# Half-row matmuls in the first feed-forward layer of a fused attention and feed-forward block

## The chip, the cores and the metric

The kernel runs on one core of a Trainium2 chip. The metric is the time of one execution on the device in microseconds (us), here the median of three runs.

## The reference

The input x has 2048 tokens (S) of 576 values (D). It is normalised per token, and the result goes to two branches that are added to x:

```python
x = A_x
xn = _layernorm(x, axis=-1)
return x + _A_ref(xn, A_wqkv, A_wo) + _B_ref(xn, B_w1, B_b1, B_w2)
```

Branch A is attention with 32 heads over 8 earlier positions at distances of 2. Branch B, in which the change lies, is a dense layer from 576 to 4608, Mish, and a dense layer back:

```python
h = jnp.einsum("bsd,df->bsf", x, w1) + b1
sp = jnp.log1p(jnp.exp(-jnp.abs(h))) + jnp.where(h > 0, h, jnp.zeros_like(h))
act = h * jnp.tanh(sp)
return jnp.einsum("bsf,fd->bsd", act, w2)
```

All inputs are float32.

## The kernel before, in words

**Precision.** A float32 operand is split into a high part, rounded to the format in which TensorE multiplies in one pass, and a low part, the difference. A product is three matmuls: high by high, low by high, high by low.

**The rest.** 576 is 4 x 128 + 64. The 64 left over are put on all 128 partitions: the host repeats the last 64 rows of the weights (`dup`, L1560), and `transpose_split` (L67) stores the transposed activations with their high part in partitions 0 to 63 and their low part in partitions 64 to 127 (L84 to L87). One matmul with the repeated high weights then gives high by high and low by high at once; a second one with the low weights gives high by low, and low by low beside it. These two matmuls are `rest` (L665 to L668).

**Halves, blocks, quads.** The tokens are done in two halves (hf) of 1024, each of two blocks (b) of 512, whose transposed activations are the tiles XTs[hf, b]: slots 0 to 3 high parts, 5 to 8 low parts, slot 4 the rest, and in block 1 also slot 9, the rest of block 0 less that of block 1. The hidden layer's 4608 columns are 36 groups of 128; a quad takes two groups and both blocks of a half, so there are 18 quads in a half and 36 in all. A quad makes its 2 x 2 blocks of h with Strassen and Winograd's seven products in place of eight: `m1_part` (L719) has six parts. Part 0 makes the first and second product, part 1 the third, parts 2 and 3 add to the first bank, part 4 finishes the third bank, part 5 the first. `prod` (L658) is one product over 256 inputs: six matmuls 512 wide. Each quad has four rests of two matmuls: in part 0 on bank 2, in part 3 on bank 1, in part 4 on bank 3, in part 5 on bank 1 (slot 9).

**Banks and evictions.** `bank` (L654) takes one of four PSUM buffers (tag h). `take` (L690) has ScalarE copy bank 1 as it then is into a tile (c11, c21 or c22; L695). `mish` (L697) puts its work off to the next item of the plan (`pend`, or `late` for the first quad): VectorE adds a bank to the copy (L706), ScalarE applies Mish (L707) and casts to the high part (L712), and GpSimd subtracts for the low part (L713). In part 3 of the kernel before, mish of block (1,1) reads bank 3, which part 4 goes on to write. In the first nine quads of the second half the results stay whole in `raw_act` slots, and a second Strassen form (`p_item`, L839) takes them up later.

**The order of work.** `plan` (L1139) is a list of items written out by hand: projections (`qkv_item`, `z_part`), first-layer parts, second-layer items (`m2_pair` L752, `p_item` L839, `m2_cols` L865) and output projections (`wo_part`). In the usual quad second-layer items of the quad before stand between parts 2, 3, 4 and 5. `quad` (L1227) has the orders; the first quad of each half takes its parts as 0, 2, 1, 3, 5, 4. Weight loads, splits and the attention's steps on the other engines are hung on items by `before` (L1148). On each engine the program order is the order of issue (L1544 to L1550).

Of the kernel before, what the change touches and what calls it, by code (L numbers as in the profile page):

```python
# [8 lines left out]
F32 = mybir.dt.float32  # L9
# [8 lines left out]
P = 128  # L18
# [21 lines left out]
def block_kernel(ctx: ExitStack, tc: tile.TileContext, x, wq, wo, w1, b1, w2, mask, out):  # L40
    nc = tc.nc
# [22 lines left out]
    for k in range(30):  # L64
        nc.tensor.transpose(warm[:, (k % 4) * P:(k % 4 + 1) * P], ident, ident)

    def transpose_split(src, dst, col, extra=None, pair=False):  # L67
        n = next(tpn)
        if pair:
            ta, tb = (ps.tile([P, 512], F32, tag="out", bufs=4, name=f"tt{k}_{n}") for k in range(2))  # L70
        else:
            ta = ps.tile([P, 512], F32, tag="h", bufs=4, name=f"ta_{n}")
            tb = ps.tile([P, 512], F32, tag="h", bufs=4, name=f"tb_{n}")
        for k in range(KT):
            nc.tensor.transpose(ta[:, k * P:(k + 1) * P], src[:, k * P:(k + 1) * P], ident)  # L75
        nc.tensor.transpose(tb[:, 0:P], src[:, KT * P:(KT + 1) * P], ident)
        if extra is not None:
            nc.tensor.transpose(tb[:, P:2 * P], extra, ident)
        tav = ta.rearrange("p (k t) -> p k t", k=KT)
        hi = dst[:, 0:KT, col:col + P]  # L80
        nc.scalar.copy(hi, tav)  # L81
        nc.vector.tensor_sub(dst[:, 5:5 + KT, col:col + P], tav, hi.bitcast(F32))
        e = 1 if extra is None else 2
        hr = dst[:, KT:KT + 5 * e - 4:5, col:col + P]  # L84
        tbv = tb.rearrange("p (k t) -> p k t", k=KT)[:, 0:e]
        nc.scalar.copy(hr, tbv)
        nc.vector.tensor_sub(hr[64:P], tbv[64:P], hr[64:P].bitcast(F32))  # L87

    XTs = {}
    rems = {}  # L90
# [93 lines left out]
    def ln_transpose(hf, b, jj):  # L184
        if jj == 0:
            XTs[hf, b] = sb.tile([P, 9 + b, TB], F32R, tag=f"xt{b}", bufs=1, name=f"xt_{hf}_{b}")
        xn = xns[hf, b * JB + jj]
        if (b, jj) == (0, 0):
            rems[hf] = sb.tile([P, JB, P], F32, tag="tt", bufs=2, name=f"rem_{hf}")
        rem = rems[hf][:, jj, :]  # L190
        if b == 0:
            nc.gpsimd.tensor_copy(rem, xn[:, KT * P:])
        else:
            nc.gpsimd.tensor_tensor(out=rem, in0=rem, in1=xn[:, KT * P:], op=ALU.subtract)
        transpose_split(xn, XTs[hf, b], jj * P, rem if b else None, (hf, b) == (1, 0) and jj < 3)

    def raw_load(src, width, name):
        raw = sb.tile([P, 5 * P], F32, tag="raw", bufs=4, name=f"r{name}")
# [452 lines left out]
    cur = {}  # L651
    late = []

    def bank(hf, q, n):  # L654
        cur[n] = ps.tile([P, TB], F32, tag="h", bufs=4, name=f"h{n}_{hf}_{q}")
        return cur[n]

    def prod(ph, wt, off, X, hi, lo, first, last):  # L658
        seq = [(off + k, wl, xs + k) for k in range(2) for wl, xs in ((0, hi), (0, lo), (1, hi))]
        for i, (wk, wl, xs) in enumerate(seq):  # L660
            nc.tensor.matmul(ph, wt[:, wl, wk * P:(wk + 1) * P], X[:, xs, :],  # L661
                             start=first and i == 0, stop=last and i == len(seq) - 1,
                             skip_group_check=True)

    def rest(ph, wt, off, X, xs):  # L665
        for wl in range(2):
            nc.tensor.matmul(ph, wt[:, wl, off * P:(off + 1) * P], X[:, xs, :], start=False, stop=wl == 1,  # L667
                             skip_group_check=True)  # L668

    seven = lambda hf, q: hf == 1 and q <= 2 * OC  # L670
# [2 lines left out]
    def raw_act(q, b, j):  # L673
        if not rslot:
            for n in range(4):
                rslot["raw", n] = sb.tile([P, 5 * P], F32, tag="raw", bufs=4, name=f"ra{n}")
            for n in range(5):
                rslot["mn", n] = sb.tile([P, D], F32, tag="mn", bufs=5, name=f"rm{n}")
            for n in range(2):
                rslot["tt", n] = sb.tile([P, 4 * P], F32, tag="tt", bufs=2, name=f"rt{n}")  # L680
        tag, n = {(0, 0): (("raw", 0), ("raw", 1), ("raw", 2)), (1, 0): (("mn", 2), ("mn", 3), ("mn", 0), ("r3", 0)),
                  (0, 1): (("raw", 3), ("mn", 4), ("mn", 1)), (1, 1): (("tt", 0), ("tt", 1))}[b, j][q % {(1, 0): 4, (1, 1): 2}.get((b, j), 3)]
        if (tag, n) not in rslot:
            rslot[tag, n] = sb.tile([P, 2 * 432], F32, tag="r3", bufs=1, name="ra_r")
        rawact[q, b, j] = rslot[tag, n][:, 0:TB]
        owner[tag, n] = q, b, j
        where[q, b, j] = tag, n
        return rawact[q, b, j]

    def take(hf, q, name):  # L690
        if seven(hf, q):
            t = cur[name] = raw_act(q, *dict(c11=(0, 0), c21=(1, 0), c22=(1, 1))[name])
        else:
            t = cur[name] = sb.tile([P, TB], F32, tag="mn", bufs=5, name=f"{name}_{hf}_{q}")
        nc.scalar.copy(t, cur[1])  # L695

    def mish(hf, q, b, j, ph, t=None):  # L697
        f = 2 * (Q1[q] if hf else q) + j
        n = f"{hf}_{b}_{f}"
        fresh = t is None  # L700
        if fresh:
            t = raw_act(q, b, j) if seven(hf, q) else sb.tile([P, TB], F32, tag="mn", bufs=5, name=f"mn_{n}")

        def run():
            if not fresh:
                nc.vector.tensor_tensor(out=t, in0=ph, in1=t, op=ALU.add)  # L706
            nc.scalar.activation(t, ph if fresh else t, AF.Mish, bias=b1c[:, f:f + 1])  # L707
            if seven(hf, q):
                held_[q, f"A{b + 1}{j + 1}"] = f"A{b + 1}{j + 1}"
                return  # L710
            a = acts[hf, q, b, j] = sb.tile([P, 2, TB], F32R, tag=f"a{b}", bufs=(3, 2)[b], name=f"act_{n}")
            nc.scalar.copy(a[:, 0, :], t)  # L712
            nc.gpsimd.tensor_tensor(out=a[:, 1, :], in0=t, in1=a[:, 0, :].bitcast(F32), op=ALU.subtract)  # L713
        if q or b != j:
            pend.append(run)
        else:
            late.append(run)

    def m1_part(hf, q, part):  # L719
        X0, X1 = XTs[hf, 0], XTs[hf, 1]  # L720
        if part == 5 and late:
            for fn in late[::-1]:
                fn()
            late.clear()
        wa, wc, t0, t1 = (done.get((k, hf, q)) for k in ("wa", "wc", "t0", "t1"))
        if part == 0:
            prod(bank(hf, q, 1), wa, 0, X0, 0, 5, True, True)
            take(hf, q, "c11")
            prod(bank(hf, q, 2), wa, 2, X0, 2, 7, True, False)
            rest(cur[2], wa, 4, X0, 4)  # L730
            mish(hf, q, 0, 0, cur[2], cur["c11"])
        elif part == 1:
            prod(bank(hf, q, 3), t1, 0, X1, 0, 5, True, True)
        elif part == 2:
            prod(cur[1], t0, 2, Ss[hf, 1], 0, 2, False, True)
            take(hf, q, "c21")
        elif part == 3:
            prod(cur[1], t0, 0, Ss[hf, 0], 0, 2, False, False)
            rest(cur[1], wc, 2, X1, 4)
            take(hf, q, "c22")  # L740
        elif part == 4:
            prod(cur[3], t1, 2, X1, 2, 7, False, False)
            rest(cur[3], wa, 4, X1, 4)
            mish(hf, q, 1, 0, cur[3], cur["c21"])
        else:
            prod(cur[1], wc, 0, Ss[hf, 2], 0, 2, False, False)
            rest(cur[1], wc, 2, X1, 9)
            mish(hf, q, 0, 1, cur[1])
        if part == 3:
            mish(hf, q, 1, 1, cur[3], cur["c22"])  # L750

    def m2_pair(hf, q, b, p):  # L752
        for jj in (2 * p, 2 * p + 1):
# [403 lines left out]
    def mi(hf, q, part, alias=None):  # L1157
        add(("m", hf, q, part), lambda: m1_part(hf, q, part), alias=alias)
# [21 lines left out]
    def prologue():  # L1180
        for ns in ((0,), (1,), (2,), (3,), (4, 5), (6, 7)):
            ln_group(ns)
        hold(ln_stats(0))
        ln_root(0)
        first_cast(0, nc.gpsimd)()
        ln_newton(0)
        ln_stats(1)
        low1 = first_cast(1, nc.gpsimd)
        ln_norm(0)
        low1()  # L1190
        first_cast(2, nc.gpsimd)()
        ln_root(1)
        ln_newton(1)
        ln_transpose(0, 0, 0)
        first_cast(3, nc.gpsimd)()
        ln_norm(1)
        first_cast(4, nc.gpsimd)()
        ln_stats(2)
# [23 lines left out]
    def tr(b, jj):  # L1222
        add(("t", 1, b, jj), lambda: ln_transpose(1, b, jj))
# [273 lines left out]
    for n in range(2 * steps):  # L1497
# [4 lines left out]
        hf = n // steps  # L1502
# [86 lines left out]
```

## Time and profile before

| What | Value |
|---|---|
| Median of 3 runs | 1120.08 us (1119.49 to 1120.12) |
| Span of the profiled execution, first to last instruction | 1118.2 us |
| Outside that span, against the median | 1.9 us |
| Granted TensorE clock | 1.000 of full speed |
| Instructions | 18402 |
| DMA, all queues | 271.08 MB, mean 242 GB/s |

The profiled execution is known by its span alone. In the page's rows PE is TensorE's matmuls, PEld its weight loads, DVE VectorE, ACT ScalarE, POOL GpSimd, SP the engine that issues the DMAs. A group of instructions is shown as line, engine, operation, output<-input, shape and count, then busy time and mean duration, then the idle time ahead of them and what ended it. A timeline row has the start, the length of the whole merged stretch, the engine, the line, the operation and the count; what stands in brackets is the idle time ahead of it and what ended that. A row of one line's instructions has the shortest, median and longest duration in ns, and the first and last start in us. Matmuls are pipelined: the next one starts before the last has ended, so the lengths of neighbouring rows overlap.

### The profile page before, as it was taken

What the parts mean: (1) busy time and instruction counts of PE and PEld (TensorE: products, weight loads), DVE (VectorE), ACT (ScalarE), POOL (GpSimd) and SP (SyncE); (2) the same over time, 40 slices, a digit from 0 to 9 for tenths busy, and PEclk for the clock granted to TensorE, in tenths of its full rate; (3) what the DMA queues carried; (4) which work ended last, traced back from release to release, by engine and by line L of the source; (5) the groups of instructions that cost most, each with busy time, mean ns of one, the idle gap of its engine ahead of it and who ended that gap; (6) DMA issues with size and microseconds to landing.
All of it is one profiled execution on the core that took longest, in us unless ns stands there. A gap on an engine that the chain in (4) does not pass through costs nothing.

```text
span 1118.2 us, 18402 instructions
## 1 busy us (share of the span) xinstructions
PE 1109.2 (99%) x6630; PEld 1023.9 (92%) x6630; DVE 835.2 (75%) x1355; ACT 491.7 (44%) x892; POOL 777.4 (70%) x631
## 2 busy tenths in 40 slices
PE   8999999999999999999999999999999999999998
PEld 8999899999999999999999888989999999999998
DVE  6369788888888888887656566687866677776876
ACT  5544645544554545555233354343433343443332
POOL 2479777767689687685787346666789878668632
PEclk9999999999999999999999999999999999999999
DMA  6899695868767849666696797665655477576463
GB/s 200 284 311 313 227 357 205 294 227 282 260 241 265 273 169 342 226 240 215 208 332 234 240 378 254 225 200 188 220 192 190 173 266 270 207 258 243 160 217 108
DMA packets 147487, 271.08 MB, mean 242 GB/s; under 512 B 30114, under 2 KB 86724, under 8 KB 147396
## 3 DMA queue, kind: packets, MB, share of 16 engines
q1 hardware_dynamic: 147396, 269.91, 69.8%
q8 instruction: 52, 0.85, 0.3%
q14 instruction: 39, 0.32, 0.1%
HBM read 160.39 MB, written 109.48 MB: 241 GB/s over the span
## 4 chain that ended last, share of the span: by engine, by line
PE 94%; DVE 3%; POOL 1%; ACT 1%; issue 1%; DMA 0%; SPq 0%; DVEq 0%; POOLq 0%; ACTq 0%
PE h L661 30%; PE po L759 20%; PE pq L348 11%; PE po L872 10%; PE po L851 7%; PE h L667 6%; PE o L1060 4%; PE z L446 4%; POOL accP L860 1%; DVE accP L875 0%; POOL act L713 0%; DMA acc<-in_x 0%; PE ta L75 0%; DVE og L582 0%; POOL act L814 0%
## 5 line engine op out<-in xcount | busy, mean ns | idle before, releaser
L759 PEld LDWEIGHTS po<-w,act 128*128 128x128 f32 x1728 | 236.4, 188 | 6.0 <-POOL act L713 0.4
L759 PE MATMUL po<-w,act 128*128 128x288 f32 x1728 | 240.7, 295 | 0.1
L576 POOL TENSOR_TENSOR pv<-L,kv 128x576 f32<-128x576 f32 x128 | 176.3, 1477 | 38.5 <-DVE L L569 28.9
L713 POOL TENSOR_TENSOR act<-c,act 128x512 fp32r<-128x512 f32 x81 | 107.6, 1329 | 126.1 <-ACT act L712 124.4
L538 POOL TENSOR_TENSOR pr<-q,kv 128x576 f32<-128x576 f32 x120 | 184.2, 1564 | 7.7 <-DMA q<-q_d 6.0
L763 DVE TENSOR_TENSOR acc<-po,acc 128x288 f32<-128x288 f32 x288 | 120.0, 449 | 31.8 <-PE po L759 30.5
L348 PE MATMUL pq<-wq,xt 128*128 128x432 f32 x672 | 136.4, 361 | 1.2 <-ACT xt L81 1.2
L872 PEld LDWEIGHTS po<-w,act 128*128 128x128 f32 x960 | 131.1, 188 | 3.7 <-DVE accP L875 0.4
L872 PE MATMUL po<-w,act 128*128 128x288 f32 x960 | 133.8, 295 | 0.2
L348 PEld LDWEIGHTS pq<-wq,xt 128*128 128x128 f32 x672 | 125.0, 188 | 8.2 <-ACT xt L81 2.1
L707 ACT ACTIVATE c<-c,b1c 128x512 f32<-128x512 f32 x81 | 58.7, 725 | 130.6 <-DVE c L706 130.2
L661 PE MATMUL h<-S,t 128*128 128x512 f32 x432 | 110.4, 391 | 0.0
L661 PE MATMUL h<-xt,t 128*128 128x512 f32 x432 | 110.4, 391 | 0.0
L695 ACT COPY c<-h 128x512 f32<-128x512 f32 x81 | 47.5, 586 | 133.2 <-PE h L667 75.2
L582 DVE TENSOR_REDUCE og<-pv 128x144 f32<-128x1152 f32 x64 | 85.9, 1343 | 26.8 <-POOL pv L576 26.7
L661 PE MATMUL h<-xt,wa 128*128 128x512 f32 x432 | 104.1, 390 | 0.0
L543 DVE TENSOR_REDUCE L<-pr 128x64 f32<-128x1152 f32 x64 | 85.8, 1342 | 17.6 <-POOL pr L538 17.4
L875 DVE TENSOR_TENSOR accP<-po,accP 128x288 f32<-128x288 f32 x160 | 69.7, 454 | 38.9 <-PE po L872 37.4
L661 PEld LDWEIGHTS h<-xt,wa 128*128 128x128 f32 x432 | 80.9, 188 | 17.0
L851 PEld LDWEIGHTS po<-pw,u 128*128 128x128 f32 x672 | 92.2, 188 | 2.9 <-DVE u L805 0.7
L851 PE MATMUL po<-pw,u 128*128 128x288 f32 x672 | 93.7, 295 | 0.4 <-DVE u L805 0.4
L661 PEld LDWEIGHTS h<-xt,t 128*128 128x128 f32 x432 | 79.1, 188 | 14.7 <-DVE rt L706 0.2
(232 smaller groups left out, 1848.7 us busy)
## 6 DMA issues: line engine op xcount, KB each, us to landing
kv<-kv_d SPq DMA_DIRECT2D x64, 396.0 KB, 5.6
kept_t<-t SPq DMA_DIRECT2D x36, 512.0 KB, 5.2
t<-kept_t SPq DMA_DIRECT2D x36, 512.0 KB, 5.0
rw<-in_w SPq DMA_DIRECT2D x36, 320.0 KB, 4.5
kept_wa<-wa SPq DMA_DIRECT2D x18, 640.0 KB, 4.7
kept_w<-w SPq DMA_DIRECT2D x20, 576.0 KB, 4.1
wa<-kept_wa SPq DMA_DIRECT2D x18, 640.0 KB, 6.3
w<-kept_w SPq DMA_DIRECT2D x20, 576.0 KB, 4.7
```

Of the source, the lines that this page charges most:

```text
L348: nc.tensor.matmul(pq[:, 0:432], XT[:, xi, tok], wt[wi][:, hl, 0:432], start=i == 0, stop=i == len(seq) - 1)
L538: nc.gpsimd.tensor_tensor(out=pr[:, x:x + hh], in0=q[:, j0 + x:j0 + x + hh, None, :].to_broadcast([P, hh, W, CU]), in1=win(kt, 0, CU, j0 + ...
L543: nc.vector.tensor_reduce(L[:, k, j0:j0 + hj].rearrange("p j w h -> p (j w h)"), pr.rearrange("p j w (h d) -> p (j w h) d", h=2), axis=AX, ...
L576: nc.gpsimd.tensor_tensor(out=pr[:, x:x + hj].rearrange("p j d w -> p j w d"), in0=L[:, k, x:x + hj, :, h:h + 1].to_broadcast([P, hj, W, DH]),
L582: nc.vector.tensor_reduce(og[:, :, c0:c0 + DH], pr, axis=AX, op=ALU.add)
L661: nc.tensor.matmul(ph, wt[:, wl, wk * P:(wk + 1) * P], X[:, xs, :], start=first and i == 0, stop=last and i == len(seq) - 1, skip_group_ch ...
L713: nc.gpsimd.tensor_tensor(out=a[:, 1, :], in0=t, in1=a[:, 0, :].bitcast(F32), op=ALU.subtract)
L759: nc.tensor.matmul(po, acts[hf, q, b, j][:, al, tok], done["w2", hf, 2 * q + j][:, wl, c * HC:(c + 1) * HC], start=i == 0, stop=i == 5)
L763: nc.vector.tensor_tensor(out=t, in0=po, in1=t, op=ALU.add)
L851: nc.tensor.matmul(po, units[e, k, qq][:, al, tok], w[:, qq, wl, :], start=i == 0, stop=i == 5)
L872: nc.tensor.matmul(po, acts[hf, q, b, j][:, al, tok], done["w2", hf, 2 * q + j][:, wl, c * HC:(c + 1) * HC], start=i == 0, stop=i == 5)
L875: nc.vector.tensor_tensor(out=t, in0=po, in1=t, op=ALU.add)
```

## The change

The rest's low-weight matmul is taken out of `rest` and done on the 64 partitions that hold the high activations, with the 64 rows of low weights on the same partitions. Two of them stand next to each other, one on partitions 0 to 63 and one on 64 to 127, and write different banks. The term low by low drops out of the rest. For the lower half to be usable, slot 4 of block 1 is stored with its low part in partitions 0 to 63 and its high part in 64 to 127; slot 9 and block 0 stay as they were. The subtraction that stores the low parts, one instruction over both slots in block 1, becomes one for each slot.

The first pair, at the end of part 3, finishes the rests of bank 2 (from part 0) and bank 1 (part 3). The second, in part 4 or 5, whichever comes first, finishes those of bank 3 and of bank 1 with slot 9; the high-weight matmul of the latter moves there too. The Mish of block (0,0), which read bank 2 after part 0, moves to part 3, ahead of that of block (1,1).

```diff
+        for n in range(e):
+            lo = slice(0, 64) if low_first and n == 0 else slice(64, P)
+            nc.vector.tensor_sub(hr[lo, n], tbv[lo, n], hr[lo, n].bitcast(F32))
-        nc.vector.tensor_sub(hr[64:P], tbv[64:P], hr[64:P].bitcast(F32))
...
+    TOP, BOT = slice(0, 64), slice(64, P)
+
     def rest(ph, wt, off, X, xs):
-        for wl in range(2):
-            nc.tensor.matmul(ph, wt[:, wl, off * P:(off + 1) * P], X[:, xs, :], start=False, stop=wl == 1,
+        nc.tensor.matmul(ph, wt[:, 0, off * P:(off + 1) * P], X[:, xs, :], start=False, stop=False,
+                         skip_group_check=True)
+
+    def rest_low(*terms):
+        for rows, ph, wt, off, X, xs in terms:
+            nc.tensor.matmul(ph, wt[rows, 1, off * P:(off + 1) * P], X[rows, xs, :], start=False, stop=True,
                              skip_group_check=True)
...
             rest(cur[2], wa, 4, X0, 4)
-            mish(hf, q, 0, 0, cur[2], cur["c11"])
...
         elif part == 3:
             prod(cur[1], t0, 0, Ss[hf, 0], 0, 2, False, False)
             rest(cur[1], wc, 2, X1, 4)
+            rest_low((TOP, cur[2], wa, 4, X0, 4), (BOT, cur[1], wc, 2, X1, 4))
+            mish(hf, q, 0, 0, cur[2], cur["c11"])
             take(hf, q, "c22")
+            mish(hf, q, 1, 1, cur[3], cur["c22"])
+            cur["rests"] = True
         elif part == 4:
             prod(cur[3], t1, 2, X1, 2, 7, False, False)
+        else:
+            prod(cur[1], wc, 0, Ss[hf, 2], 0, 2, False, False)
+        if part > 3 and cur["rests"]:
+            cur["rests"] = False
             rest(cur[3], wa, 4, X1, 4)
+            rest(cur[1], wc, 2, X1, 9)
+            rest_low((BOT, cur[3], wa, 4, X1, 4), (TOP, cur[1], wc, 2, X1, 9))
+        if part == 4:
             mish(hf, q, 1, 0, cur[3], cur["c21"])
-        else:
-            prod(cur[1], wc, 0, Ss[hf, 2], 0, 2, False, False)
-            rest(cur[1], wc, 2, X1, 9)
+        if part == 5:
             mish(hf, q, 0, 1, cur[1])
-        if part == 3:
-            mish(hf, q, 1, 1, cur[3], cur["c22"])
```

More of the change, by code (lines that the diff above doesn't have):

```diff
@@ L65, in block_kernel, with transpose_split @@
         nc.tensor.transpose(warm[:, (k % 4) * P:(k % 4 + 1) * P], ident, ident)
-    def transpose_split(src, dst, col, extra=None, pair=False):
+    def transpose_split(src, dst, col, extra=None, pair=False, low_first=False):
         n = next(tpn)
@@ L194, in ln_transpose @@
             nc.gpsimd.tensor_tensor(out=rem, in0=rem, in1=xn[:, KT * P:], op=ALU.subtract)
-        transpose_split(xn, XTs[hf, b], jj * P, rem if b else None, (hf, b) == (1, 0) and jj < 3)
+        transpose_split(xn, XTs[hf, b], jj * P, rem if b else None, (hf, b) == (1, 0) and jj < 3, b == 1)
     def raw_load(src, width, name):
@@ L739, in m1_part @@
             rest(cur[1], wc, 2, X1, 4)
+            rest_low((TOP, cur[2], wa, 4, X0, 4), (BOT, cur[1], wc, 2, X1, 4))
+            mish(hf, q, 0, 0, cur[2], cur["c11"])
             take(hf, q, "c22")
+            mish(hf, q, 1, 1, cur[3], cur["c22"])
+            cur["rests"] = True
         elif part == 4:
             prod(cur[3], t1, 2, X1, 2, 7, False, False)
-            rest(cur[3], wa, 4, X1, 4)
-            mish(hf, q, 1, 0, cur[3], cur["c21"])
         else:
             prod(cur[1], wc, 0, Ss[hf, 2], 0, 2, False, False)
+        if part > 3 and cur["rests"]:
+            cur["rests"] = False
+            rest(cur[3], wa, 4, X1, 4)
             rest(cur[1], wc, 2, X1, 9)
+            rest_low((BOT, cur[3], wa, 4, X1, 4), (TOP, cur[1], wc, 2, X1, 9))
+        if part == 4:
+            mish(hf, q, 1, 0, cur[3], cur["c21"])
+        if part == 5:
             mish(hf, q, 0, 1, cur[1])
-        if part == 3:
-            mish(hf, q, 1, 1, cur[3], cur["c22"])
     def m2_pair(hf, q, b, p):
```

## Prediction

> **What bounds the kernel now.** I read the page's busy shares and slices first, then the list of waits, then the chain of work that ended last. They answer in that order whether an engine is full, whether it ever stands still, and which of its lines make up the time.
>
> ```profile
> span 1118.2 us, 18402 instructions
> PE 1109.2 (99%) x6630; PEld 1023.9 (92%) x6630; DVE 835.2 (75%) x1355; ACT 491.7 (44%) x892; POOL 777.4 (70%) x631
> PEclk9999999999999999999999999999999999999999
> PE warm L65 <- POOL ident masks.py:199: 1.3, 1, 1.3
> PE po L851 <- DVE u L805: 0.4, 1, 0.4
> PE 94%; DVE 3%; POOL 1%; ACT 1%; issue 1%; DMA 0%; SPq 0%; DVEq 0%; POOLq 0%; ACTq 0%
> PE h L661 30%; PE po L759 20%; PE pq L348 11%; PE po L872 10%; PE po L851 7%; PE h L667 6%; PE o L1060 4%; PE z L446 4%; POOL accP L860 1%; DVE accP L875 0%; POOL act L713 0%; DMA acc<-in_x 0%; PE ta L75 0%; DVE og L582 0%; POOL act L814 0%
> ```
>
> TensorE is busy 99% of the span at the full granted clock; its waits for others are single events of about a microsecond, and 94% of the chain is matmuls. So the time is the sum of the distances from one matmul's start to the next, and any matmul that goes, or runs beside another, shortens it. The line that the change touches, the 64-row rest (L667), holds 6% of the chain.
>
> What one such matmul takes must be read from starts, not from durations, because matmuls overlap. The timeline in the middle of the first half, around two rests of one quad, first TensorE's matmuls, then its weight loads, then ScalarE and VectorE:
>
> ```profile
> 296.34 1.53 PE L661 MATMUL h<-S,t 128*128 128x512 f32 x6
> 297.71 0.61 PE L667 MATMUL h<-xt,wc 128*128 128x512 f32 x2
> 298.16 3.34 PE L759 MATMUL po<-w,act 128*128 128x288 f32 x24
> 301.34 1.53 PE L661 MATMUL h<-xt,t 128*128 128x512 f32 x6
> 302.71 0.62 PE L667 MATMUL h<-xt,wa 128*128 128x512 f32 x2
> 303.16 0.42 PE L759 MATMUL po<-w,act 128*128 128x288 f32 x2
> ...
> 301.20 1.24 PEld L661 LDWEIGHTS h<-xt,t 128*128 128x128 f32 x6
> 302.48 0.41 PEld L667 LDWEIGHTS h<-xt,wa 128*128 128x128 f32 x2
> ...
> 298.36 0.59 ACT L695 COPY c<-h 128x512 f32<-128x512 f32 x1 [0.42 <-PE h L667]
> 299.71 0.72 ACT L707 ACTIVATE c<-c,b1c 128x512 f32<-128x512 f32 x1 [0.76 <-DVE c L706]
> ...
> 298.98 0.69 DVE L706 TENSOR_TENSOR c<-h,c 128x512 f32<-128x512 f32 x1
> ```
>
> Eight 512-wide matmuls start between 301.34 and 303.16: 1.82/8 = 0.227 us each. The 24 of 288 columns take (301.34-298.16)/24 = 0.132 us each. The rest's first weight load starts at 302.48, and the sixth matmul before it at 301.34 + 5 x 0.227 = 302.48 too: a load begins when the matmul ahead of its own begins, one ahead, and lies wholly under it. The second rest matmul of the earlier pair ends by its row at 297.71 + 0.61 = 298.32, and ScalarE, which had waited 0.42 us for it, starts at 298.36: a matmul's result really is there about 0.39 us after its start, though the next has long begun.
>
> **The change, part by part.** *Pairs.*
>
> ```profile
> L667 PE MATMUL h<-xt,wa x144: 388/389/397, 103.4 to 1029.0; 128*128 128x512 f32 x144
> L667 PE MATMUL h<-xt,wc x144: 388/390/405, 107.9 to 1034.0; 128*128 128x512 f32 x144
> ```
>
> These are 288 rest matmuls: four rests of two (high weights, low weights) in each of 36 quads. The 144 with low weights now use 64 rows each and stand in 72 pairs, one on the upper half of the rows and one on the lower, into different banks of PSUM. A pair costs 2 x 0.227 = 0.454 us now. No matmul of this trace uses 64 rows, so the pair's price is bounded. From above, as a plain sequence: 0.454, nothing won. From below, both at once: 0.227, which wins 72 x 0.227 = 16.3 us. Between lies what the rows suggest: two matmuls on different rows can stream together, but the lower one's weights are loaded one ahead, that is from the upper one's start. How soon a matmul can follow the start of its load is bounded by the densest streams of the trace: 0.132 us by the 288-wide matmuls above, and less by transposes:
>
> ```profile
> 1039.82 0.96 PE L872 MATMUL po<-w,act 128*128 128x288 f32 x6
> 1040.61 0.60 PE L906 MATMUL ot<-ident,o 128*128 128x128 f32 x4
> 1041.05 0.60 PE L922 MATMUL ot<-ident,o 128*128 128x128 f32 x4
> ```
>
> Four transposes take 1041.05 - 1040.61 = 0.44 us, 0.110 each. I take 0.132, the row with the same kind of operands. Then the lower half starts 0.132 after the upper, the next full matmul 0.227 behind that, the pair costs 0.359, and 72 x (0.454 - 0.359) = 6.8 us go. By the transposes it is 72 x (0.454 - 0.337) = 8.4 us.
>
> *Change of rows.* TensorE now goes from 128 rows to 64 and back around every pair, 144 times. The nearest row is the change from matmul to transpose above: 6 matmuls from 1039.82 to 1040.61 take 0.132 each, so that change costs nothing. I take nothing. It could cost as much as a wait for the last result, 0.39 us from a start and not 0.227, or that and a weight load behind it; this end is the rival on the other side.
>
> *The first output block's activation moves* from the quad's first part to its fourth. Nothing of it is new: one VectorE addition, one activation, one cast, one GpSimd subtraction. But the addition now stands ahead of the one for block (1,1) (L706), which frees the bank that the next product writes. In the rows above ScalarE's copy ends at 298.95, the addition runs from 298.98 to 299.67, and the product starts at 301.34: 1.67 us to spare. The addition put in front, 0.69 us, can begin at 298.36, while ScalarE still copies, and so delays the other by only 0.1 us. Where VectorE has a queue it delays it in full; the second quad is such a place:
>
> ```profile
> 127.18 1.36 DVE L255 TENSOR_TENSOR w<-rw,w 128x576 fp32r<-128x576 f32 x1
> 128.47 0.68 DVE L706 TENSOR_TENSOR c<-h,c 128x512 f32<-128x512 f32 x1
> 126.09 3.08 PE L759 MATMUL po<-w,act 128*128 128x288 f32 x22
> ```
>
> There the addition ends at 129.15 and the stream of 22 that covers it at 126.09 + 22 x 0.132 = 129.0, so about 0.55 us are lost. If every quad lost the whole 0.69 us it would be 25 us, but that needs the cover gone: what hides it is the 3.2 us of second-layer matmuls between parts. Three quads have none there, and two of these have projection matmuls in its place. I take 0.5 us in all, between 0 and 2. The bank of the first block is held longer, but its next user comes a quad later.
>
> *The other new wait*: the fourth rest now writes its bank in part 4 instead of 5, behind ScalarE's copy (L695). The copy ends at 298.95, the rest comes after 302.71: 3.7 us to spare. Taken at nothing; behind it on TensorE would stand everything.
>
> *The rest stored low part first.*
>
> ```profile
> L87 DVE TENSOR_TENSOR xt<-tb,xt x13: 294/427/428, 10.4 to 558.0; 64x256 fp32r<-64x256 f32 x8, 64x128 fp32r<-64x128 f32 x5
> ```
>
> Eight subtractions of 64x256 become two of 64x128 each: 8 x (2 x 0.295 - 0.427) = 1.3 us more on VectorE, spread over eight transposes, and no engine waits for this line. Nothing. No DMA is added, and SP's queue keeps its order.
>
> **Sum.** The median of the runs is 1120.1 us, the profiled execution's span 1118.2, so 1.9 lie around it and stay. 1120.1 - 6.8 + 0.5 = 1113.8.
>
> **The rivals.** *The halves start together.* If the lower half's load is not held behind the upper matmul, both loads fit under the full matmul ahead, 2 x 0.110 = 0.22 of its 0.227 us, and the pair costs 0.227: 1120.1 - 16.3 + 0.5 = 1104.3. For it: each half has its own rows to load. Against it: every load in the rows starts no more than one matmul ahead. The Trainium skill ("TensorE: Matmul & The Clock Gate", Part 3, "The mechanism") says that loads to other row groups are pulled ahead and the starts then lie about 4 ns apart; no run here shows it yet.
>
> *The pair is a sequence.* Then the change does not do what it says: a matmul of 64 rows streams the same 512 columns, and the time stays at 1120.1 to 1120.6.
>
> *A pause at each change of rows.* If TensorE lets the full matmul finish before a 64-row one starts, and the reverse, the time is longer. With the weights loaded meanwhile: the upper half starts 0.390 after the full matmul's start and the lower between 0 and 0.132 behind it, the next full one 0.390 behind that, 0.780 to 0.912 in place of 3 x 0.227 = 0.681. That is 0.10 to 0.23 us more a pair, 7 to 17 us: 1127.7 to 1137, the middle 1132. If the load, too, waits for the pause, each of the two changes adds another 0.110 to 0.132: 23 to 36 us, 1143 to 1156, the middle 1150. The price decides: at the forecast's overlap the pair wins 0.095, so that a pause of over 0.048 us at each change makes the kernel slower; with halves that start together the point is 0.113. For it: a full matmul's sums pass all the rows on which the next one wants to start afresh, and nothing in this trace shows such a change. Against it: the change to transposes is free. The Trainium skill ("TensorEngine Tiling (Array Packing)", "Key Properties") has a sentence that speaks for it: "Changing tiling mode (not just tile) drains the TensorE". It gives no duration, and no run so far shows it.
>
> **How the numbers follow.** A measurement of this kernel tells about 0.2%, 2.2 us, from no change. Chances: the forecast 0.27 (1111.5 to 1115.5); halves together 0.24 (1104.3); sequence 0.06 (1120.1); pause with loads ahead 0.23 (1132); pause with loads behind 0.20 (1150). Faster is 0.51, same 0.06, slower 0.43. The range begins just under the second case, at 1103. To end at 1137 would leave out 0.20 and the edges of the others; it goes to the middle of the last case, 1150, and leaves out about half of that.
>
> **What would show it.** Each of the 144 low matmuls must show 64 rows. In the timeline around a pair: starts of upper, lower and next full matmul at 0, 0.132 and 0.359 us are the forecast; 0, under 0.02 and 0.23 the first rival; 0, 0.227, 0.454 the second. The distance from the high-weight matmul to the upper half is 0.227 if a change of rows is free, 0.39 or over if it pauses; a weight load that starts behind the end of the matmul before it would show the last case. TensorE's waits for L706 should grow by under 2 us. The distances of all other matmuls, 0.132 and 0.227, should stay; if they don't, or if TensorE comes to wait for block (0,0)'s activation, my account of the rest of the kernel is wrong.

## The result and the profile after

The changed kernel takes 1133.39 us (median of 4 runs, 1133.31 to 1133.45), beside 1119.83 us for the kernel before on the same chip (1119.49 to 1120.12): the ratio is 1.0122, with a 95% interval of 1.0108 to 1.0136. It is 13.6 us slower where 6.3 us faster was forecast. The page of the changed kernel, in the order in which that of the kernel before was read:

```profile
span 1131.6 us, 18391 instructions
PE 1121.1 (99%) x6630; PEld 1003.3 (89%) x6630; DVE 844.7 (75%) x1363; ACT 488.3 (43%) x892; POOL 776.0 (69%) x631
PEclk9999999999999999999999999999999999999999
PE 94%; DVE 3%; POOL 1%; ACT 1%; issue 1%; DMA 0%; SPq 0%; DVEq 0%; POOLq 0%
PE h L663 29%; PE po L773 21%; PE pq L350 11%; PE po L886 10%; PE po L865 7%; PE o L1074 4%; PE z L448 3%; PE h L670 3%; PE h L675 3%; POOL accP L874 1%; DVE accP L889 1%; POOL act L721 0%; DMA acc<-in_x 0%; PE ta L75 0%; DVE og L584 0%
```

TensorE is as full as before and on the same clock, though its busy time grew by 11.9 us while 72 slots of a matmul should have gone. The first two lines of the list of waits of TensorE, and then of its weight loads, tell where to look:

```profile
PE ta L75 <- ACT xn L182: 1.7, 2, 1.3
PE o L1074 <- DVE y L1078: 1.6, 2, 1.0
...
PEld h L675 <- issue: 26.0, 72, 0.4
PEld po L773 <- issue: 6.8, 28, 0.2
```

TensorE's matmuls wait for other engines about as little as before (the whole list adds up to 6.7 us, that of the kernel before to 5.3). But the weight loads stood still 72 times for 26.0 us ahead of the pairs (L675), once in each, and what ended it was no other engine ("issue"). The timeline around the second pair of the quad that the prediction showed, matmuls first and then loads, and the row of the pairs' matmuls:

```profile
304.51 1.53 PE L663 MATMUL h<-xt,t 128*128 128x512 f32 x6
305.88 0.39 PE L670 MATMUL h<-xt,wa 128*128 128x512 f32 x1
306.10 0.39 PE L670 MATMUL h<-xt,wc 128*128 128x512 f32 x1
306.42 0.49 PE L675 MATMUL h<-xt,wa 64*128 64x512 f32 x1
306.42 0.49 PE L675 MATMUL h<-xt,wc 64*128 64x512 f32 x1
306.85 3.46 PE L773 MATMUL po<-w,act 128*128 128x288 f32 x24
310.14 1.53 PE L663 MATMUL h<-S,wc 128*128 128x512 f32 x6
...
305.88 0.19 PEld L670 LDWEIGHTS h<-xt,wc 128*128 128x128 f32 x1
306.42 0.18 PEld L675 LDWEIGHTS h<-xt,wa 64*128 64x128 f32 x1 [0.35 <-issue]
306.42 0.18 PEld L675 LDWEIGHTS h<-xt,wc 64*128 64x128 f32 x1
306.84 3.22 PEld L773 LDWEIGHTS po<-w,act 128*128 128x128 f32 x24 [0.24 <-issue]
...
L675 PE MATMUL h<-xt,wa x72: 491/498/502, 107.8 to 1042.2; 64*128 64x512 f32 x72
```

The two halves do start together, loads and matmuls alike. The price stands on both sides of them. Between full matmuls a load starts with the matmul ahead of its own. Here both loads start at 306.42, 0.32 us after the full matmul's start at 306.10, where the next would have started after 0.227: a pause of 0.09 us. And the pair's matmuls have their start recorded with that of their loads and last 0.498 in place of 0.389 us: the load of 0.11 us, hidden elsewhere, now lies bare in front of them. On the way back it is the same: the next load starts at 306.84, 0.42 us behind the pair's recorded start, which is again 0.11 of bare load and 0.31. The 24 matmuls then take 310.14 - 306.85 = 3.29 us and not 24 x 0.132 = 3.17, the bare load of the first.

So, by these rows, a change of rows costs 0.09 + 0.11 = 0.20 us, there are two around each pair, and the pair saves one slot of 0.227: 2 x 0.20 - 0.227 = 0.173 us lost in each, 12.5 us in 72.

### The profile page after: what moved, and what is told of

Same layout as the page of the kernel before. It is cut to its first block, busy times and chain, and to the rows that moved or that the text cites. A ratio compares the mean times of both kernels' runs of the same rounds, so it can differ in the third digit from the quotient of the medians.

```text
span 1131.6 us, 18391 instructions
## 1 busy us (share of the span) xinstructions
PE 1121.1 (99%) x6630; PEld 1003.3 (89%) x6630; DVE 844.7 (75%) x1363; ACT 488.3 (43%) x892; POOL 776.0 (69%) x631
## 4 chain that ended last, share of the span: by engine, by line
PE 94%; DVE 3%; POOL 1%; ACT 1%; issue 1%; DMA 0%; SPq 0%; DVEq 0%; POOLq 0%
PE h L663 29%; PE po L773 21%; PE pq L350 11%; PE po L886 10%; PE po L865 7%; PE o L1074 4%; PE z L448 3%; PE h L670 3%; PE h L675 3%; POOL accP L874 1%; DVE accP L889 1%; POOL act L721 0%; DMA acc<-in_x 0%; PE ta L75 0%; DVE og L584 0%
## 5 line engine op out<-in xcount | busy, mean ns | idle before, releaser
L773 PE MATMUL po<-w,act 128*128 128x288 f32 x1728 | 244.6, 297 | 0.1
L773 PEld LDWEIGHTS po<-w,act 128*128 128x128 f32 x1728 | 233.9, 188 | 11.7 <-issue 6.8
L777 DVE TENSOR_TENSOR acc<-po,acc 128x288 f32<-128x288 f32 x288 | 123.9, 451 | 44.5 <-PE po L773 43.1
L886 PE MATMUL po<-w,act 128*128 128x288 f32 x960 | 135.7, 297 | 0.4 <-POOL act L828 0.3
L886 PEld LDWEIGHTS po<-w,act 128*128 128x128 f32 x960 | 129.7, 188 | 6.7 <-issue 1.7
L663 PEld LDWEIGHTS h<-S,t 128*128 128x128 f32 x432 | 77.9, 188 | 12.8
```

The source lines that it names most:

```text
L773: nc.tensor.matmul(po, acts[hf, q, b, j][:, al, tok], done["w2", hf, 2 * q + j][:, wl, c * HC:(c + 1) * HC], start=i == 0, stop=i == 5)
L777: nc.vector.tensor_tensor(out=t, in0=po, in1=t, op=ALU.add)
L886: nc.tensor.matmul(po, acts[hf, q, b, j][:, al, tok], done["w2", hf, 2 * q + j][:, wl, c * HC:(c + 1) * HC], start=i == 0, stop=i == 5)
```

## The experiments

The theory: each change between full matmuls and 64-row ones costs about 0.2 us, and hardly anything else in the change costs time. The rivals: the moved activation and its waits cost it; the 64-row matmuls themselves are dear.

**The order alone.** Every low-weight matmul on 128 rows, all else as changed.

```diff
-        for rows, ph, wt, off, X, xs in terms:
+        for _, ph, wt, off, X, xs in terms:
+            rows = slice(0, P)
```

> The changed kernel with its order, its pairs and its moved activation, but every low-weight matmul on all 128 rows. Theory (each change of rows costs TensorE about 0.2 us: 0.09 us of pause and 0.11 us of a weight load that nothing covers; the rest of the change costs nothing): no change of rows is left, so 1119.8 to 1121. Rival (the moved activation of block (0,0), the moved rest and their waits cost the time): about 1133.

Measured: 1120.92 us, 1.0009 of the kernel before (0.9999 to 1.0019). The moved activation, the moved rest and the divided subtraction together cost 1.1 us, with an interval from -0.1 to 2.1: they are not the cause. What the half rows add to this is 1133.39 - 1120.92 = 12.5 us, or 0.173 a pair, the sum worked out above.

**Each pair twice.**

```diff
-        for rows, ph, wt, off, X, xs in terms:
+        for rows, ph, wt, off, X, xs in terms + terms:
```

> The changed kernel with each pair issued twice in a row (the low terms are added twice, so this is not the reference's sum). Theory: no further change of rows, only 72 more slots of a 512-wide matmul, 72 x 0.227 = 16.3 us over the changed kernel: 1149.7. Rival (the cost belongs to each 64-row matmul or pair, not to the change of rows): each added pair costs its slot of 0.227 and 0.174 us and the lost overlap again, 72 x 0.4 to 72 x 0.63 = 29 to 45 us: 1162 to 1179.

Measured: 1151.25 us, 1.0278 (1.0263 to 1.0293). The 72 added pairs cost 17.9 us over the changed kernel, 0.248 each; the slots alone make 0.227, and the 0.02 us between them lie within the intervals of the two runs. The timeline of this run, matmuls and then loads:

```profile
304.47 0.39 PE L670 MATMUL h<-xt,wc 128*128 128x512 f32 x1
304.79 0.49 PE L675 MATMUL h<-xt,wa 64*128 64x512 f32 x1
304.80 0.49 PE L675 MATMUL h<-xt,wc 64*128 64x512 f32 x1
305.13 0.39 PE L675 MATMUL h<-xt,wa 64*128 64x512 f32 x1
305.13 0.39 PE L675 MATMUL h<-xt,wc 64*128 64x512 f32 x1
305.45 3.45 PE L773 MATMUL po<-w,act 128*128 128x288 f32 x24
...
304.90 0.19 PEld L675 LDWEIGHTS h<-xt,wa 64*128 64x128 f32 x1
304.90 0.19 PEld L675 LDWEIGHTS h<-xt,wc 64*128 64x128 f32 x1
```

The second pair's loads start 0.11 us after the first pair's record, that is with its stream, and are covered; its matmuls last the usual 0.39 us. From the first pair to the next full matmul it is 305.45 - 304.79 = 0.66 us in place of 0.43: one slot more. Within 64 rows nothing is lost, so the price is the change's, not the matmul's.

**Alone at the old place.** In the kernel before, each low-weight matmul on the upper 64 rows.

```diff
-        for wl in range(2):
-            nc.tensor.matmul(ph, wt[:, wl, off * P:(off + 1) * P], X[:, xs, :], start=False, stop=wl == 1,
+        for wl, r in ((0, P), (1, 64)):
+            nc.tensor.matmul(ph, wt[0:r, wl, off * P:(off + 1) * P], X[0:r, xs, :], start=False, stop=wl == 1,
```

> The kernel before, its order untouched, with each of the 144 low-weight matmuls on the upper 64 rows alone, at its old place (low by low drops out of the rest, as in the changed kernel). Theory: 288 changes of rows at 0.2 us and no overlap to win: 1119.8 + 57.6 = 1177. Rival (each 64-row matmul has a price of its own, 0.174/2 us): 1132. Rival (the moved work costs the time): 1120.

Measured: 1176.89 us, 1.0508 (1.0492 to 1.0524). Over 1119.86 that is 57.0 us for 288 changes, 0.198 each, with the old order of everything. Both rivals fall: one gave 1132, the other 1120.

**Both on one half.**

```diff
-        transpose_split(xn, XTs[hf, b], jj * P, rem if b else None, (hf, b) == (1, 0) and jj < 3, b == 1)
+        transpose_split(xn, XTs[hf, b], jj * P, rem if b else None, (hf, b) == (1, 0) and jj < 3)
...
-    TOP, BOT = slice(0, 64), slice(64, P)
+    TOP, BOT = slice(0, 64), slice(0, 64)
```

> The changed kernel with block 1's rest stored high part first everywhere and both matmuls of a pair on the upper 64 rows. Theory: the two can't overlap, the changes of rows stay: 72 x 0.224 = 16.1 us over the changed kernel, 1149.5, with starts about 0.23 us apart within the pair. Rival (the halves do not really run together; the equal starts in the trace are only how they are recorded): 1133, as the changed kernel.

Measured: 1150.13 us, 1.0271 (1.0255 to 1.0286); 16.7 us over the changed kernel. In this run's timeline the same pair reads:

```profile
304.19 0.39 PE L670 MATMUL h<-xt,wc 128*128 128x512 f32 x1
304.51 0.49 PE L675 MATMUL h<-xt,wa 64*128 64x512 f32 x1
304.85 0.39 PE L675 MATMUL h<-xt,wc 64*128 64x512 f32 x1
305.17 3.46 PE L773 MATMUL po<-w,act 128*128 128x288 f32 x24
```

The second starts 0.34 us behind the first's record, 0.11 of bare load and a slot of 0.23. So in the changed kernel the two halves really run beside each other, and the overlap is worth 0.23 us a pair, as the best case had it.

**The first pair of each quad alone** on half rows, the second on all 128.

```diff
-            rest_low((BOT, cur[3], wa, 4, X1, 4), (TOP, cur[1], wc, 2, X1, 9))
+            ALL = slice(0, P)
+            rest_low((ALL, cur[3], wa, 4, X1, 4), (ALL, cur[1], wc, 2, X1, 9))
```

> The changed kernel with the second pair of each quad on all 128 rows, the first left on 64. Theory: half of the changes of rows, half of the loss: 1119.8 + 6.8 = 1126.6. Rival (one of the two places carries the cost, by a wait there): 1120 or 1133.

Measured: 1127.44 us, 1.0070 (1.0055 to 1.0085). It lies between the order alone, 1120.92, and the changed kernel, 1133.39: 6.5 of 12.5 us, half for half of the changes. No single place carries the cost.

**A narrow matmul ahead of the pair.**

```diff
-        nc.tensor.matmul(ph, wt[:, 0, off * P:(off + 1) * P], X[:, xs, :], start=False, stop=False,
-                         skip_group_check=True)
+        for c in (slice(0, 256), slice(256, TB)):
+            nc.tensor.matmul(ph[:, c], wt[:, 0, off * P:(off + 1) * P], X[:, xs, c], start=False, stop=False,
+                             skip_group_check=True)
```

> The changed kernel with each high-weight rest matmul cut into two of 256 columns, so that a matmul half as wide stands ahead of each pair. The cut itself costs 144 x (2 x 0.13 - 0.227) = about 4.8 us. Theory A (the pause is counted from the end of the stream ahead): the pair's weight loads start about 0.21 us after the last narrow matmul's start and the time is about 1138. Theory B (the pause runs to a fixed time from that matmul's start, as 0.32 us in the changed kernel): 0.32 us, and about 1146.

Measured: 1136.03 us, 1.0144 (1.0127 to 1.0161). That is nearer to theory A, and the timeline, the pair's load and the narrow matmul's row decide it:

```profile
306.85 0.40 PE L671 MATMUL h<-xt,wc 128*128 128x256 f32 x2
307.18 0.50 PE L676 MATMUL h<-xt,wa 64*128 64x512 f32 x1
307.19 0.50 PE L676 MATMUL h<-xt,wc 64*128 64x512 f32 x1
...
307.18 0.18 PEld L676 LDWEIGHTS h<-xt,wa 64*128 64x128 f32 x1
...
L671 PE MATMUL h<-xt,wc x144: 277/281/288, 107.8 to 1044.3; 128*128 128x256 f32 x144
```

The two narrow matmuls end at 306.85 + 0.40 = 307.25, and one lasts 0.28, so the last one starts at 306.97 and the pair's loads 0.21 us behind it, not 0.32. With 256 columns fewer ahead, the pause begins 0.11 us sooner: at these two widths it is counted from the end of the stream ahead and not from its start. The forecast times were too long because a narrow matmul takes 0.12 us here, not 0.13: the cut costs 144 x (2 x 0.12 - 0.227) = about 1.9 us and not 4.8. Theory A then gives about 1135 and theory B, 0.11 us more for each of 72 pairs, about 1143; measured are 1136.03.

**96 and 32 rows.** As with the lone matmuls, with another number of rows.

```diff
-        for wl, r in ((0, P), (1, 64)):
+        for wl, r in ((0, P), (1, 96)):
```

> As the run with each low-weight matmul alone at its old place, but on 96 rows in place of 64 (of low by low, half stays). Theory A (every change in the number of rows costs the 0.2 us): 1177, as with 64 rows. Theory B (only a matmul that takes the array in halves or quarters does; 96 rows is issued as a full one): 1120. Which of the two holds was left open by the runs so far.

> The same on 32 rows (this leaves out half of the high by low of the rest). Theory A and B both: 288 changes at 0.2 us, 1177. Rival (the price grows or falls with the rows that are left idle): by more than 10 us away from that.

Measured: 1123.23 us with 96 rows, 1.0032 (1.0020 to 1.0044), and 1178.03 with 32, 1.0522 (1.0504 to 1.0541). The timelines of the 96-row run, with the row of half of its rest matmuls, and of the 32-row run (a merged row bears the shape of its first matmul; the second of each two is the one on 96 or 32 rows):

```profile
296.40 1.53 PE L661 MATMUL h<-S,t 128*128 128x512 f32 x6
297.77 0.62 PE L667 MATMUL h<-xt,wc 128*128 128x512 f32 x2
298.23 3.35 PE L759 MATMUL po<-w,act 128*128 128x288 f32 x24
...
L667 PE MATMUL h<-xt,wa x144: 389/394/398, 102.8 to 1031.6; 128*128 128x512 f32 x72, 96*128 96x512 f32 x72
```

```profile
295.88 0.82 PE L667 MATMUL h<-xt,wc 128*128 128x512 f32 x2
296.63 3.02 PE L661 MATMUL h<-xt,wa 128*128 128x512 f32 x12
299.49 0.81 PE L667 MATMUL h<-xt,wa 128*128 128x512 f32 x2
```

With 96 rows the two rest matmuls take 298.23 - 297.77 = 0.46 us, nearly as full ones do (0.45), and none lasts 0.498. With 32 rows it is 0.75, and the 12 matmuls behind take 299.49 - 296.63 = 2.86 us and not 12 x 0.227 = 2.72: there the next load is bare as well. So of the three numbers of rows that were run, 64 and 32 make a change, 96 does not, and 32 costs what 64 does. Some 3.6 us, 0.025 a matmul, come with the 96 rows even so. In that run's trace the matmul behind a 96-row one starts 0.233 us after it (median) and not 0.227, which makes 0.9 of them; the others stay open.

## Why the prediction was wrong, point by point

- *What bounds the kernel*: right. Each 0.2 us added to TensorE's row of matmuls came out in the time, 0.198 by the lone matmuls.
- *Change of rows: "I take nothing."* This step failed, and it alone turned the sign. The change to transposes, taken as the nearest row, costs nothing, but it is no change of rows: its lines say 128*128 on both sides. The change to 64 rows costs 0.20 us, 144 times, 28.8 us in all. The price from which the kernel becomes slower was put at 0.048 us, or 0.113 with halves that start together; 0.20 is past both. What happens is the rival of a pause with the weight loads behind it, which was given 0.20. Its mechanism was right, its size, 23 to 36 us, too big: it let TensorE wait until the last result is there, 0.39 us after a start, but the next load starts after 0.32, about 0.1 us behind the end of the stream, and it let the lower half start up to 0.132 us late. The signs named for it do not fit the rows as they were worded: from the high-weight matmul to the upper half's record it is 0.32 us, between the 0.227 and the 0.39 of the prediction, and the load starts behind the end of the stream ahead (306.10 + 0.227) but not behind the end of that matmul's row (306.10 + 0.39). The milder rival, a pause with the loads ahead (1127.7 to 1137, chance 0.23), has the measured 1133.39 within its bounds by luck: the loads lie bare, and its upper bound came from a lower half that starts late, which it does not. The Trainium skill ("TensorEngine Tiling (Array Packing)", "Key Properties") says that changing the tiling mode drains TensorE. These traces agree, and add its price here, a pause of 0.09 us and the bare load of 0.11.
- *The lower half waits for its load, 0.132 us*: wrong, on the other side. Both loads start at 306.42 and both matmuls with them, so a pair of slots shrinks to one: 16.3 us are won, not 6.8. That is the first rival's half of the matter. The two together: 28.8 - 16.3 = 12.5. The Trainium skill ("TensorE: Matmul & The Clock Gate", Part 3, "The mechanism") puts starts on different rows about 4 ns apart. The trace agrees: the recorded starts of a pair lie 3 to 4 ns apart in all 72.
- *The moved activation, 0.5 us, between 0 and 2*: 1.1 for all that was moved, by the run with full rows, with an interval that holds 0.5. The example behind it was wrong, though. The stream of 22 that covers the addition was cut off by the end of the window, at 129 us; it has 24 matmuls and lasts to 129.28, where the product starts, so the addition that ends at 129.15 was 0.13 us early. (With an end at 129.0 it would have been late already, and the 0.55 would not follow.) And VectorE's queue lay elsewhere after the change. In the second quad of the changed kernel VectorE and TensorE read:

```profile
125.91 1.35 DVE L257 TENSOR_TENSOR w<-rw,w 128x576 fp32r<-128x576 f32 x1
127.18 1.27 DVE L714 TENSOR_TENSOR c<-h,c 128x512 f32<-128x512 f32 x2
...
126.34 3.46 PE L773 MATMUL po<-w,act 128*128 128x288 f32 x24
129.64 1.53 PE L663 MATMUL h<-xt,t 128*128 128x512 f32 x6
```

The work ahead of the additions starts at 125.91 and no longer at 127.18. Both are over by 127.18 + 1.27 = 128.45, well ahead of the product at 129.64; no stall of 0.55 us came.
- *The fourth rest behind ScalarE's copy, and the divided subtraction*: neither shows among TensorE's waits, as forecast.
- *The range*, 1103 to 1150, holds the time, because the rivals' bounds were taken in; the likeliest case and the sign were wrong.

## What to carry to other kernels

Two matmuls on 64 rows each can share one slot, but going to 64 rows and back costs two changes of 0.20 us here, so a stretch of n pairs of 512-wide matmuls between full ones wins about 0.227 n - 0.40 us. This is an estimate from the 0.227 and the 0.20 above: one pair loses 0.17, two barely win 0.05, and only longer stretches pay. The run with each pair twice bears out the second: four full matmuls in each place would make 1120.92 + 144 x 0.227 = about 1153.6 us, and it took 1151.25, so each stretch of two pairs won about 0.03, barely clear of the intervals. Longer stretches were not run. Before packing rows, count the changes between full and 64-row matmuls, not only the matmuls that go. And when a trace has no row for a step that happens 144 times, work out the price at which the sign turns, here 0.05 us a step, before a price of nothing goes into the sum.

## What had not been expected of the hardware

A matmul on 96 rows stands among full ones without the pause (0.46 us for the two rest matmuls); one on 32 pays the same as one on 64 (1178.03 and 1176.89 us). The pause does not last until the result ahead has arrived, 0.39 us after the start; it ends 0.32 after the start of a 512-wide matmul and 0.21 after that of a 256-wide one, about 0.1 us behind the end of its stream. And where a load is bare, the record of the matmul starts with that of its load, so its 0.498 us are read as 0.11 of load and 0.389 of matmul; the second matmul in the run with both on one half, 0.11 + 0.23 us behind the first's record, bears this out.
